# RWKV-5 attention and a tanh-shrink layer on one core: how many blocks of tokens take the early passes

## The chip, the core and the metric

The kernel runs on one core of a Trainium2 chip. A core has a matrix engine (PE, with its weight loads shown apart as PEld), a vector engine (DVE), an activation engine (ACT), a general engine (POOL), and SP, which here only issues transfers. Each runs its own list of instructions in order; semaphores tie them together. The metric is the device time of one launch in microseconds (us); lower is better.

## The reference

Three inputs r, k and v of 4 batches x 8 heads x 768 steps x 48, a decay w and a bonus u per head and channel, and two weight matrices.

```python
for t in range(S):
    kt, vt, rt = (k[:, :, t], v[:, :, t], r[:, :, t])
    cur = np.einsum('bhd,bhe->bhde', u[None] * kt, vt)
    y[:, :, t] = np.einsum('bhd,bhde->bhe', rt, state + cur)
    state = w[None, :, :, None] * state + np.einsum('bhd,bhe->bhde', kt, vt)
...
x = np.ascontiguousarray(attn_out.transpose(0, 2, 1, 3)).reshape(B * S, H * D)
h = x @ w_in
g = h - np.tanh(h)
return (g @ w_out).astype(np.float32)
```

x is 3072 x 384, w_in 384 x 2048, w_out 2048 x 384. The activations are fp32; w_in and w_out arrive as 64-bit floats, which the kernel converts itself.

## The kernel before, in words

**The work.** The attention is computed in 24 *units*, each 64 steps of two batches. Two units (L = 2) give 256 tokens, one *block* of the dense layer: 12 blocks. The dense layer's 2048 inner columns are cut into 16 slices f of 128, taken in pairs: a *tile* is one block with one pair of slices, and there are 12 x 8 = 96 tiles.

- **A unit** (`unit`, inside `near`): SP fetches r, k and v in six transfers (L730); DVE multiplies k by a decay table (kw, L871); PE transposes r and kw (L742); DVE scales r (rT, L746) and ACT copies k (kT, L755); PE multiplies rT with the running state and with kT (L697); DVE masks the result into `at` (L896), whose diagonal ACT has written (L767) from a product of r and k summed on DVE (L759, L886, L763); PE makes the outputs and the state's update (L697); ACT copies the outputs to the block's `xt` (L833); DVE updates the state (L860, L905). Some rows reach `xt` by six small transfers from POOL (L854).
- **A tile** (`hidden`): PE makes h in two halves of six matmul records (L167, `Dense.h`); ACT makes five functions of it (L176 to L184); DVE makes g in four steps (L191, L193, L195, L197); then PE multiplies g by w_out.
- **Plain or seven.** That last product is either four plain fp32 matmuls of 384 columns (L205, `Dense.o`), or a scheme of seven products of 192 columns (L255, `products`), as in Strassen's method. The seven need sums of g, which POOL makes (L240 to L244), and *mixed* sums of w_out, which DVE makes once all weights are converted (L264, `mix`). After a block's last seven-product tile the seven results are put together in seven steps, one on ACT (L274) and six on DVE (L283, `collect`), with the buffers e, u and o.
- **Weights.** 16 *pieces* (`Weights`), half of w_in and half of w_out, each 768 KB in HBM: loaded by SP and POOL (L122), converted by five steps on DVE (L136, L137, L140 to L142) and two on ACT (L138, L139). Every fourth pair of slices needs four pieces.

**The order of blocks.** All weights can't be there at the start. So the first FIRST = 5 blocks go through the dense layer in three *passes* over f, PASSES = 4, 4, 8 slices: two tiles of each of the five blocks, then again two of each, then four of each. The first two passes are plain and their sums are kept (`part`, L218 and L229); the third takes seven products and adds the kept sum (`gather`, L287). The other blocks, 5 to 11, go one after another with all eight tiles in seven products, but for the very last tile, which is plain.

The units of blocks 0 to FIRST + 1 (the first 14) use two banks of PSUM of their own (x_ps); units from 14 on (`two` in the code) share one pair of banks, and their product with the state is a step apart, followed by a small copy on ACT. The first seven-product tile needs the last of the first 14 units, since the seven results take over the x_ps banks.

**What sets the order of instructions.** `Plan` takes each step with an engine, a cost in us, and what it waits for. A fixed-seed search over due times fills an order per engine; the kernel issues exactly that order. Transfers carry another figure, `data`, the time for which each occupies the transfer channel: 3.0 for a w_out piece, 1.2 and 0.8 for the parts of a w_in piece on SP and POOL, 0.62 for half of a unit's r, k or v. Loads of weights are issued no sooner than 45 us before they are due (`gated`). Where the plan leaves PE idle before the first h and before the first o, *fillers* are put in (L632, a matmul of the identity with itself, in 512 or 256 columns). The plan also counts PE's instructions and expects PE to wait for its own at every 256.

**Buffers.** `xt` has FIRST + 2 buffers and `part` 2 x FIRST. In `collect`, e and u have 384 columns each, of which u uses 192; `kU`, used by unit 0 alone, lies in the buffers of `rk`.

Of the kernel before, what the change touches and what calls it, by code (L numbers as in the profile page):

```python
# [11 lines left out]
F32 = mybir.dt.float32  # L12
# [18 lines left out]
SHORT = 64  # L31
# [1 line left out]
PAD = 64  # L33
AHEAD = 2
L = 2
FIRST = 5
PASSES = 4, 4, 8
OWN = 1
SWAP = 2
# [105 lines left out]
class Dense:  # L145
# [62 lines left out]
    def empty(self, t, i):  # L208
# [13 lines left out]
        else:  # L222
            t.o = self.sums[at] = self.work.tile([128, self.d.DM], F32, name="part", tag="part", bufs=L * FIRST)
        if t.j == self.d.NB - 1:
# [41 lines left out]
    def collect(self, t, x):  # L266

        n, ps, V = self.d.DM // 2, self.seven.ps, self.nc.vector
        if x == 0:
            t.e, t.u = (self.work.tile([128, self.d.DM], F32, name=name, tag=name, bufs=1) for name in "eu")  # L270
            t.os = [self.work.tile([128, self.d.DM], F32, name="o", tag="o") for _ in range(L)]
            if t.fs[1] < self.d.NF:
                self.sums.update({(t.j, i): t.os[i] for i in range(L)})
            self.nc.scalar.copy(t.e[:, :n], ps[0][:, :n])  # L274
        else:
            o, e, u = t.os, t.e, t.u[:, :n]
            out, x, y, op = [(e[:, n:], e[:, :n], ps[0][:, n : 2 * n], ALU.subtract),
                             (u, e[:, n:], ps[1][:, n : 2 * n], ALU.add),
                             (o[1][:, :n], u, ps[1][:, :n], ALU.add),
                             (o[1][:, n:], u, ps[2][:, n : 2 * n], ALU.add),  # L280
                             (o[0], e, ps[2][:, : 2 * n], ALU.add),
                             (o[0][:, n:], o[0][:, n:], ps[3][:, :n], ALU.add)][x - 1]
            V.tensor_tensor(out, x, y, op)  # L283
# [15 lines left out]
class Plan:  # L299
# [7 lines left out]
    HOP, NEAR_HOP, LANDS, LANDED, LANES, EARLY, SPARE, WARM, SLOW = 0.16, 0.06, 2.4, 1.6, 8, 45.0, 20.0, 6.0, (60.0, 3.0)  # L307
    CHUNK, CHUNK_0, ASKED, COMES, FIRST = 256, 192, 55, 3.4, 9.5
    BEGIN = {"PE": 1.5, "DVE": 2.2, "ACT": 1.2, "POOL": 4.3, "SP": 1.2}
# [4 lines left out]
    def add(self, engine, cost, run, after=(), due=1e9, data=0, gated=False, steps=0):  # L314
        t = SimpleNamespace(engine=engine, cost=cost, run=run, after=[x for x in after if x], due=due, data=data,
                            gated=gated, steps=steps, then=[], n=len(self.tasks))
        for x in t.after:
            x.then.append(t)
        self.tasks.append(t)
        return t  # L320
# [12 lines left out]
    def forward(self, due):  # L333

        ready = [max(self.FIRST, due[t.n] - self.EARLY) if t.gated else 0.0 for t in self.tasks]
        count = [len(t.after) for t in self.tasks]
# [157 lines left out]
def near(ctx, tc, r, k, v, w, u, out, shared, moe_w_in, moe_w_out):  # L494
# [5 lines left out]
    H, D, NP, NK, B, HEAD = d.H, d.D, d.NP, d.NK, d.B, d.HEAD  # L500
# [4 lines left out]
    work = ctx.enter_context(tc.tile_pool(name="n_work", bufs=2))  # L505
# [10 lines left out]
    add = plan.add  # L516
# [149 lines left out]
    def steps(generator):  # L666

        made = []

        def step():  # L670
            if not made:
                made.append(generator())
            next(made[0])

        return step

    loads, converted = [], []
    for n in range(weights.count):

        queues, data = (("SP",), (3.0,)) if n % 4 > 1 else (("SP", "POOL") * 2, (1.2, .8) * 2)  # L680
        of = [add(e, .55, lambda n=n, i=i, e=e: weights.load(n, i, e_of[e]), [converted[n - 4] if n >= 4 else None],
                  data=x, gated=True) for i, (e, x) in enumerate(zip(queues, data))]
        if weights.sources[n % 4 > 1].dtype != I64:
            converted.append(of[-1])
            continue
        step = steps(lambda n=n: weights.convert(n))
        now = of + ([converted[n - 2]] if n >= 2 else [])
        for name, cost in (("DVE", .47), ("DVE", .47), ("ACT", .84), ("ACT", .84), ("DVE", .87), ("DVE", .87), ("DVE", .87)):
            now = [add(name, cost, step, now)]
        converted += now  # L690
# [10 lines left out]
    def unit(n):  # L701
# [6 lines left out]
        t = SimpleNamespace(at=ats[n % 2])  # L708
        rt, vt, kw, state = rts[n % (AHEAD + 1)], vts[n % (AHEAD + 1)], kws[n % 2], states[half]
        two = n >= L * (FIRST + 2)  # L710
        pair = yk_ps if two else x_banks[n == 1]
# [13 lines left out]
        def fetch(name, src, after):  # L725
            def run(z):
                if name == "k" and not hasattr(t, "kt"):
                    t.kt = first_k[slot] if direct else load.tile([128, H, D], F32, name="kt", tag="kt")
                to = {"r": rt, "v": vt}.get(name)
                Q.dma_start(out=(t.kt if to is None else to)[HALF[z], :, :D],  # L730
                            in_=src[half * 2 + z, :, steps_at, :].rearrange("h t d -> t h d"))

            of = [add("SP", .65, lambda z=z: run(z), after, data=.62) for z in range(2)]
            return add("none", 0, lambda: None, of)

        x.r = fetch("r", r, [b3.turn, b3.rk, b1.r])
        x.k = fetch("k", k, [b3.kw, b3.rk, b1.k])
        x.v = fetch("v", v, [b3.out, b1.v])

        def turn(src, to):  # L740
# [26 lines left out]
                A.mul(t.at[:, h % 2, h // 2], same, t.du[:, h : h + 1])  # L767

        def own_k():
            t.kU = work.tile([128, NP, 2, SHORT], F32, name="kU", tag="rk")  # L770
            for p in range(NP):
                A.mul(t.kU[:, p], t.kT[:, p], w_u[:, p : p + 1])

# [56 lines left out]
        def given(out, y):  # L830

            def copy(out, y):
                A.copy(out, y) if sign > 0 else A.activation(out, y, AF.Copy, scale=sign)  # L833

            if not swap:
                copy(out, y)
                return
            copy(out[:, 0], y[:, 0])
            for i in range(2):
                copy(out[i * PAD : (i + 1) * PAD, 1], y[to(i, 1), 1])  # L840

        def to_xt():
            if slot == 0:
                dense.xts[j] = work.tile([128, NK, L, C], F32, name="xt", tag="xt", bufs=FIRST + 2)
            given(dense.xts[j][:, :, slot].rearrange("e p (z t) -> e z p t", z=2), y_ps[:, :, :NK])
# [34 lines left out]
        if product:  # L880
            now = add("ACT", 1.05, own_k, [x.kT, w_us])
            x.own = add("PE", .7, own_levels, [now, x.rT, b2.out], steps=64)
            x.diag = add("DVE", .64, lambda: V.copy_predicated(t.at, same.bitcast(I32)[:, None, None, :].to_broadcast([128, 2, NP, SHORT]), own_lev), [x.own, b2.out])
        else:
            x.rk = add("DVE", .47, own, [x.r, x.k, b2.du, b1.rk if not b1.own else None])
            now = add("DVE", .47, lambda: V.tensor_tensor(t.rk, t.rk, ub, ALU.mult), [x.rk, bonus])  # L886
            x.du = add("DVE", .47, own_sum, [now, b2.diag])
            now = add("ACT", 1.0, lambda: diagonal(range(0, H // 2)), [x.du, b2.out])
            x.diag = add("ACT", 1.0, lambda: diagonal(range(H // 2, H)), [now])
# [9 lines left out]
        if direct:  # L899
            now = x.out = add("PE", .6, to_state, [now, x.kw], steps=64)  # L900
        x.xt = add("ACT", .96 if swap else .4, to_xt, [now, last_h.get(j - FIRST - 2) if slot == 0 else None])
        if not direct:
# [362 lines left out]
def kernel(  # L1265
# [29 lines left out]
    with tc.manual_schedule():  # L1295
        near(tc, r, k, v, w, u, out, shared, moe_w_in, moe_w_out)
# [39 lines left out]
```

## Time and profile before

| | |
|---|---|
| runs, us | 610.80, 610.86, 612.87 (median 610.86) |
| profiled execution | 610.4 us, of which the span of instructions is 608.7 |
| mean clock granted to PE | 0.992 |
| busy us: PE, PEld, DVE, ACT, POOL | 584.0, 497.8, 465.0, 403.4, 211.3 |
| PE's groups | h 1152 records, seven products 1050, plain o 168 (of 21 tiles), units 3200 with the transposes |
| read from HBM, written | 26.94 MB, 4.72 MB |

An fp32 matmul leaves two records in the profile, so h of one tile is 12 records. Matmuls overlap in the records: the ends are modelled, and the time from one start to the next tells more than a duration. Times within a profile are counted from the start of the span. "Issue" is a wait that nothing in the profile ended.

### The profile page before, as it was taken

The page shows a single profiled execution, that of the slowest core. Times are in us where ns is not written, and L with a number is a line of the kernel's source. Part 1 is how long each engine was busy: PE and PEld are TensorE (multiplying, and loading weights), DVE is VectorE, ACT ScalarE, POOL GpSimd, SP SyncE. Part 2 cuts the span into 40 slices and gives each one's busy share as a digit, 9 for nine tenths or more (in the row PEclk, how much of TensorE's full clock was granted, in tenths as well). Part 3 has the DMA queues.
Part 4 walks back from the last instruction along what each step waited for, and adds up shares of the span by engine and source line. Part 5 has one row for each costly group of instructions (what it writes and reads, how often), then busy time and mean ns, then how long its engine had stood idle before and what let it go on. Part 6 is the DMA issues. An engine that isn't in the chain of part 4 may idle for free.

```text
span 608.7 us, 14333 instructions
## 1 busy us (share of the span) xinstructions
PE 584.0 (96%) x5617; PEld 497.8 (82%) x5617; DVE 465.0 (76%) x771; ACT 403.4 (66%) x902; POOL 211.3 (35%) x384
## 2 busy tenths in 40 slices
PE   9789889999999989999999999999999999999994
PEld 5466667777777979999999888999889989899993
DVE  4789999999999999777765856875766875646753
ACT  2478979887786565666665765865676575765552
POOL 5001122010013454555463442453424432444430
PEclk9799999999999999999999999999999999999998
DMA  7998867653012020011020221310121100100101
GB/s 126 215 160 143 198 120 114 170 103 106 13 28 46 1 41 6 20 26 27 12 49 14 51 47 18 65 34 14 34 41 27 33 9 8 28 3 5 26 1 32
DMA packets 86325, 33.77 MB, mean 55 GB/s; under 512 B 78536, under 2 KB 80680, under 8 KB 86248
## 3 DMA queue, kind: packets, MB, share of 16 engines
q1 hardware_dynamic: 81084, 25.57, 22.2%
q0 software_dynamic: 4992, 6.99, 5.4%
q8 instruction: 46, 0.75, 0.5%
q14 instruction: 31, 0.25, 0.2%
q10 hardware_dynamic: 172, 0.20, 0.1%
HBM read 26.94 MB, written 4.72 MB: 52 GB/s over the span
## 4 chain that ended last, share of the span: by engine, by line
PE 69%; DVE 12%; ACT 8%; issue 7%; POOL 1%; DMA 1%; DVEq 0%; POOLq 0%; ACTq 0%
PE h L167 32%; PE p L255 24%; PE yk_ps L697 4%; PE o L205 4%; PE h L632 2%; DVE tg L193 1%; DVE tg L195 1%; DVE g L197 1%; DVE rT L746 1%; DVE g L191 1%; ACT th L178 1%; PE yk_ps L742 1%; ACT at L767 1%; POOL xt L854 1%; ACT s L176 1%
## 5 line engine op out<-in xcount | busy, mean ns | idle before, releaser
L167 PE MATMUL h<-xt,w_in_sb 128*128 128x256 f32 x1152 | 282.4, 382 | 0.1
L167 PEld LDWEIGHTS h<-xt,w_in_sb 128*128 128x128 f32 x1152 | 212.5, 190 | 30.1 <-issue 0.7
L240 POOL TENSOR_TENSOR sg<-g 128x256 f32<-128x256 f32 x75 | 57.0, 759 | 197.6 <-DVE g L197 142.6
L191 DVE TENSOR_TENSOR g<-h,th 128x512 f32<-128x512 f32 x96 | 66.2, 689 | 60.6 <-ACT s L176 26.8
L255 PE MATMUL p<-mixed,sg 128*128 128x192 f32 x450 | 110.1, 326 | 0.0
L180 ACT ACTIVATE tg<-h 128x512 f32<-128x512 f32 x96 | 57.3, 597 | 62.3 <-PE h L167 62.3
L193 DVE SCALAR_TENSOR_TENSOR tg<-s,tg 128x512 f32<-128x512 f32 x96 | 69.6, 725 | 25.1 <-ACT tg L180 13.8
L176 ACT ACTIVATE s<-h 128x512 f32<-128x512 f32 x96 | 57.6, 600 | 38.5 <-PE h L167 37.7
L178 ACT ACTIVATE th<-h 128x512 f32<-128x512 f32 x96 | 57.1, 595 | 37.7 <-PE h L167 37.7
L255 PEld LDWEIGHTS p<-mixed,sg 128*128 128x128 f32 x450 | 79.3, 190 | 0.2 <-issue 0.2
L255 PE MATMUL p<-w_out_sb,g 128*128 128x192 f32 x300 | 74.9, 332 | 1.3 <-DVE e L283 0.9
L197 DVE COPY_PREDICATED g<-small,tg 128x512 f32<-128x512 int32 x96 | 71.2, 742 | 4.3
L195 DVE SCALAR_TENSOR_TENSOR tg<-q,tg 128x512 f32<-128x512 f32 x96 | 68.7, 716 | 6.5 <-ACT q L182 2.3
L182 ACT ACTIVATE q<-s,m1b 128x512 f32<-128x512 f32 x96 | 69.6, 725 | 0.8
L184 ACT ACTIVATE small<-s,smallb 128x512 f32<-128x512 f32 x96 | 69.4, 723 | 0.5
L854 POOL DMA_DIRECT2D xt<-rest x66 | 32.1, 493 | 106.0 <-ACT rest L833 105.5
L255 PEld LDWEIGHTS p<-w_out_sb,g 128*128 128x128 f32 x300 | 54.9, 190 | 9.5 <-DVE e L283 1.3
L205 PE MATMUL o<-w_out_sb,g 128*128 128x384 f32 x160 | 59.1, 492 | 2.0 <-DVE g L197 1.2
L767 ACT ACTIVATE at<-same,du 128x64 f32<-128x64 f32 x184 | 47.5, 342 | 7.1 <-DVE du L763 7.0
L244 POOL TENSOR_TENSOR sg<-sg,g 128x128 f32<-128x128 f32 x75 | 44.4, 592 | 5.4
L205 PEld LDWEIGHTS o<-w_out_sb,g 128*128 128x128 f32 x160 | 29.3, 190 | 15.7 <-PE x_ps L632 1.6
L242 POOL TENSOR_TENSOR sg<-sg,g 128x128 f32<-128x128 f32 x75 | 40.2, 535 | 5.4
(129 smaller groups left out, 703.6 us busy)
## 6 DMA issues: line engine op xcount, KB each, us to landing
st<-in_moe_w_out_dram SPq DMA_DIRECT2D x8, 768.0 KB, 6.8
rt<-in_r_dram SPq DMA_DIRECT2D x48, 96.0 KB, 3.2
vt<-in_v_dram SPq DMA_DIRECT2D x48, 96.0 KB, 3.1
st<-in_moe_w_in_dram SPq DMA_DIRECT2D x16, 288.0 KB, 5.5
kt<-in_k_dram SPq DMA_DIRECT2D x44, 96.0 KB, 4.6
out_dram<-o POOLq DMA_DIRECT2D x44, 96.0 KB, 2.1
st<-in_moe_w_in_dram POOLq DMA_DIRECT2D x16, 96.0 KB, 5.7
xt<-rest POOLq DMA_DIRECT2D x66, 16.0 KB, 2.1
```

The lines of the kernel that those rows point to most:

```text
L167: self.nc.tensor.matmul(t.h2[:, z], self.w_in_sb[:, t.f // 2, kk, z * 128 : (z + 1) * 128], self.xts[t.j][:, kk].rearrange("p b t -> p (b ...
L176: A.activation(out, t.h, AF.Square)
L178: A.activation(out, t.h, AF.Tanh)
L180: A.activation(out, t.h, AF.Tanh, scale=G1)
L182: A.activation(out, t.s, AF.Square, bias=self.m1b)
L184: A.activation(out, t.s, AF.Relu, bias=self.smallb, scale=-1.0)
L191: V.tensor_tensor(t.g, t.h, t.th, ALU.subtract)
L193: V.scalar_tensor_tensor(t.tg, t.s, C4, t.tg, ALU.mult, ALU.mult)
L195: V.scalar_tensor_tensor(t.tg, t.q, K1, t.tg, ALU.add, ALU.mult)
L197: V.copy_predicated(t.g, t.small.bitcast(I32), t.tg)
L205: self.nc.tensor.matmul(self.outs[i], t.g2[:, z, i * C : (i + 1) * C], self.w_out_sb[:, t.f + z, :], start=t.first and z == 0, stop=t.last ...
L255: self.nc.tensor.matmul(ps[bank][:, half * n : (half + 1) * n], a, b, start=t.first and half == 0, stop=t.last, skip_group_check=True)
```

## The change

FIRST becomes 6: six blocks go through the three passes, and 16 units use the early banks. The tiles of the sixth block with f 0 to 6 thereby become plain and their sums are kept and gathered. `u` shrinks to the 192 columns in use (e keeps its 384), and `kU` moves from rk's buffers to q's. In the planner, half of a unit's r, k or v counts 0.71 us of the channel, and POOL's part of a w_in piece 0.95. The search runs with the same seed over the new steps, and the order that it returns is another from the first instructions on.

```diff
-FIRST = 5
+FIRST = 6
 PASSES = 4, 4, 8
...
         if x == 0:
-            t.e, t.u = (self.work.tile([128, self.d.DM], F32, name=name, tag=name, bufs=1) for name in "eu")
+            t.e, t.u = (self.work.tile([128, w], F32, name=name, tag=name, bufs=1) for name, w in (("e", 2 * n), ("u", n)))
...
-            o, e, u = t.os, t.e, t.u[:, :n]
+            o, e, u = t.os, t.e, t.u
...
-        queues, data = (("SP",), (3.0,)) if n % 4 > 1 else (("SP", "POOL") * 2, (1.2, .8) * 2)
+        queues, data = (("SP",), (3.0,)) if n % 4 > 1 else (("SP", "POOL") * 2, (1.2, .95) * 2)
...
-            of = [add("SP", .65, lambda z=z: run(z), after, data=.62) for z in range(2)]
+            of = [add("SP", .65, lambda z=z: run(z), after, data=.71) for z in range(2)]
...
-            t.kU = work.tile([128, NP, 2, SHORT], F32, name="kU", tag="rk")
+            t.kU = work.tile([128, NP, 2, SHORT], F32, name="kU", tag="q")
```

## The prediction

> **What bounds the kernel now.** I read the page's slices first, then the engines' busy time by stretch.
>
> ```profile
> PE   9789889999999989999999999999999999999994
> DVE  4789999999999999777765856875766875646753
> PEclk9799999999999999999999999999999999999998
> DMA  7998867653012020011020221310121100100101
> ```
>
> PE is at 9 nearly everywhere; the digits below 9 lie in the first six slices (15.2 us each) and in the last. DVE is at 9 up to slice 15 and then falls to 5 to 8: two regimes. The stretches (columns: length, then PE, PEld, DVE, ACT, POOL busy with counts, granted clock, DMA share, GB/s):
>
> ```profile
> 20.00:30.00 10.00, 7.04 (x94) 5.14 (x95) 6.26 (x11) 3.53 (x9) 1.01 (x2) 0.66 1.10 236
> ...
> 60.00:80.00 20.00, 16.79 (x344) 11.88 (x337) 19.40 (x36) 18.85 (x54) 2.88 (x6) 1.00 0.77 175
> 80.00:100.00 20.00, 18.77 (x320) 14.65 (x320) 18.08 (x31) 16.33 (x41) 4.93 (x10) 1.00 0.83 138
> 100.00:120.00 20.00, 19.66 (x261) 14.76 (x261) 19.85 (x35) 17.78 (x49) 2.92 (x6) 1.00 0.64 150
> ...
> 160.00:180.00 20.00, 20.00 (x144) 15.12 (x143) 20.00 (x33) 15.65 (x28) 0.00 (x0) 1.00 0.07 13
> ```
>
> From 110 us on, PE never stops for long: what counts there is the PE work itself. From 60 to 110 us DVE is full and PE waits for it, 4.8 us in all. Before that everything waits in turn: loads, DVE, and once PE's own instructions. PE in order of time there:
>
> ```profile
> 18.50 0.70 PE L632 MATMUL h<-ident 128*128 128x512 f32 x1
> 22.96 1.22 PE L632 MATMUL h<-ident 128*128 128x512 f32 x1 [3.76 <-issue]
> 24.11 0.92 PE L697 MATMUL yk_ps<-at,vt 64*64 64x64 f32 x24
> ```
>
> A single filler matmul is cut in two by a stop of 3.76 us that no engine ended, and the group behind it takes 0.92 us instead of the 0.58 of its first run: the clock stands at 0.50 for 6.8 us. ACT waits 6.0 us for the transposes behind this (kT L755 from PE x_ps L742), and DVE's rT waits for that.
>
> The price of a dense tile, from two places where PE runs without a gap (PE in order of time, then the chain):
>
> ```profile
> 137.25 1.46 PE L167 MATMUL h<-xt,w_in_sb 128*128 128x256 f32 x6
> 138.54 1.45 PE L205 MATMUL o<-w_out_sb,g 128*128 128x384 f32 x4
> 139.83 1.46 PE L167 MATMUL h<-xt,w_in_sb 128*128 128x256 f32 x6
> ```
>
> ```profile
> 254.22 1.29 PE h L167 x6
> 255.51 1.30 PE p L255 x8
> 256.81 1.29 PE h L167 x6
> 259.08 1.29 PE h L167 x6
> ```
>
> Starts count, since the ends overlap: a half of h or of a plain o is 1.29, so a plain tile is 5.17 us; a seven-product tile steps from 254.22 to 259.08, 4.86 us.
>
> [...] idle from 19.2 to 22.96, clock 0.50 from 21.6 to 28.4. [...] The trace has 46 such packets in 0.75 MB[...]; the second came at 19.9 us, amid a DMA share of 1.1, and was not hidden. [...]
>
> **The change part by part.** The order of instructions is fixed when the program is built, so I compare the two orders.
>
> *PE's work.* Four tiles (one block, f 8 to 14 unchanged, f 0 to 6 now plain) go from seven products to plain: 4 x (5.17 - 4.86) = +1.25 us. Units 14 and 15 now use the early layout, in which the groups with rT stand together: a joined pair costs 1.30 us between dense halves (156.63 to 157.82, and 0.11 in the next half), two single ones 0.83 each (330.16 to 330.88, and 0.11): 2 x -0.35 = -0.7. Fillers: 11 of 512 and 1 of 256 columns on h before, 7 and 5 after; 5 and 3 on x_ps before, 8 and 2 after: 18 and 18.5 of 512 altogether, nothing. PE's work: **+0.6 us**, all on the path.
>
> *What DVE lets PE do.* I summed DVE's instructions by their mean durations up to the copy_predicated (L197) that ends each tile's g; and PE's, without fillers, up to the first o of the same tile (0.216 us per h matmul of 256 columns, 0.324 per o, 0.52 to 0.56 per group of 32, 0.5 per four transposes). A tile costs DVE 2.87, a unit 5.03, a converted piece 4.00. Before, tile 1 ends at 50.45 with a sum of 39.3 and tile 12 at 136.33 with 136.9: DVE passes 1 us of sum in 0.88, neighbours overlapping. With that rate and the start as now, the tiles after end at 50.45 + 0.88 (sum - 39.3). "Lost" is the time at which o starts less PE's work ahead of it; after, its least value.
>
> ```
> tile  before: DVE sum, PE sum, o starts, lost | after: DVE sum, ends, PE sum, lost at least
>  1            39.3     19.3    50.6      31.3 |        43.2   53.9   22.4     31.7
>  2            48.7     32.0    64.2      32.2 |        54.9   64.2   30.8     33.6
>  4            71.7     42.7    78.4      35.7 |        72.6   79.8   46.1     33.9
>  8           112.1     76.9   115.8      38.9 |       109.7  112.4   79.6     33.0
> 11           131.9     94.3   133.4      39.1 |       133.1  133.0   98.4     34.8
> 16           162.4    122.5   161.8      39.3 |       161.3  157.8  126.7     31.3
> ```
>
> Before, lost time grows to 39.1 and stays: PE is saturated. After, DVE holds PE to 34.8 at most: six blocks draw 12 tiles from the first four pieces, so at tile 8 five pieces are converted instead of eight, and PE has more of the units behind it. Up to 4.3 us can go. But PE also waits for unit steps (1.8 us for state L860, 0.8 for at L767), and more units come early; before, lost time grew 7.8 between tiles 1 and 9, while the floor after grows 3.1. I take **-3.0 us**; bounds 0 (all of it becomes waits on units) and -4.3.
>
> *The start.* SP now issues w's rows first, not fourth (0.8 us instead of 3.0). The decay table follows them, so unit 0 can start up to 3 us earlier. But piece 0's conversion waits for its load, which landed at 19.34, the moment DVE took it; the loads ahead of it are the same to one. What can move is unit 2: its rT ran at 28.27, held by the stop and the slow clock, while its r had landed by 23.3. Counted through the orders, the stop falls after 220 matmul records; after the change that is still among the fillers ahead of unit 1's outputs, but with 2.5 fillers of 512 run instead of a half, 1.7 us more cover, and the block is asked for earlier if unit 0 is earlier. Without the stop, rT could run at about 24.5 to 25.5: with 0.9 us more DVE work ahead of it, up to 4.4 us of DVE's lead. The trace doesn't show whether PE, waiting for r until 23, loses its clock all the same. I take **-2.0**; bounds -4.4, and +3.4 if a stop of the same kind comes later (half of 6.8 us at half clock).
>
> *Costed at nothing.* Smaller e and u, kU in q's buffers: no instruction changes; q's last reader there is the scan at 8.8 us. DVE gains two adds (L218, 0.574) and two gathers (L287, 0.693), ACT two copies (0.475), all beside saturated PE; were PE to wait for them, 3.5 us. POOL loses 12 additions (7.5 us), and has room. The DMA figures act through the order alone: second-pass pieces are issued later on SP, behind seven more units' loads, whose buffers come free as units pass; DVE asks for them later too.
>
> Sum: 608.7 + 0.6 - 3.0 - 2.0 = 604.3 span. The profiled run took 610.4 for 608.7, so 606.0; the median of the runs stands 0.5 above it: **606.5**.
>
> **Rivals.** (1) *The stop goes wholly*: -4.4 instead of -2.0, so 604.1. For: the boundary has more before it and is asked for earlier. Against: r of unit 2 lands at 23 anyway. (2) *The lead is not used*: PE's waits for units replace those for g, and the start stays: only PE's +0.6 is left, 611.5. For: lost time grew in 60 to 80 us, where ACT is at 18.85 of 20 as well, and units are denser there after. (3) *Slower: the second pass's weights come late.* Piece 4 stands on SP behind unit 11's k, whose buffer waits for unit 8's kw on DVE, by the sums at about 73 us; it lands 5.5 us (the page's median for these loads) or more later, at about 80, and DVE reaches its conversion at about 87. If it slips by more than these 7 us, DVE stops in its queue with the tiles' steps behind it, and PE with it, each us one us: slower than now from 4.4 us beyond, and at 10 beyond, 606.5 + 10 = 616.5. For: a load of the first 30 us took up to 11.6 us to land. Against: DMA share is 0.8 there, and later loads than before leave the early ones room.
>
> **How the numbers follow.** Forecast (603.5 to 609): 0.45. Rival 1: 0.2; rival 2: 0.15; rival 3: 0.2. A measurement can tell about 0.5%, 3.1 us, so faster is below 607.8: three quarters of the forecast and rival 1, 0.53; same, 0.27, the rest and rival 2; slower, 0.2, rival 3. The range, 600.5 to 615.5, takes in the start's -4.4 with DVE's -4.3 at its low end and reaches toward rival 3 at its high end, since only two in ten may be left out.
>
> **What would show it.** Right: no gap over 0.5 us on PE from 70 us on until the first products; o of tile 8 starting near PE's sum plus 36; rT of unit 2 by 26 us. Rival 1: clock at 1.00 through 20 to 30 us. Rival 2: PE waiting for at or state at 60 to 110 us as much as now. Rival 3: L136 waiting for st. The forecast is wrong if the time from the first seven products to the end differs by more than the four tiles' 19.4 us and the units account for.

## The result, and the profile after

| | before | after |
|---|---|---|
| runs, us | 610.80, 610.86, 612.16, 612.87 (median 611.51) | 604.17, 604.63, 606.31, 606.58 (median 605.47) |
| profiled execution, its span, us | 610.4, 608.7 | 606.31, 604.5 |
| mean clock granted to PE there | 0.992 | 0.993 |

The ratio is 0.9898, 95% interval 0.9866 to 0.9929: about 6 us off. The profiled spans differ by 4.2. The runs of the changed kernel come in two pairs, at 604.2 to 604.6 us with a mean clock of 0.996 and at 606.3 to 606.6 with 0.993. The stretch at half clock in this profile takes 3.4 us (39.6 to 43.0), and 3.4 / 2 / 605 is 0.003 of mean clock, so one such stretch more or less would account for 1.7 of the 2 us; only an execution of the upper pair was profiled, so this is not shown. All times here are of fast executions: beside f1 to f4 below, two of the kernel before (625 and 861 us, mean clock 0.942 and 0.655) and two of f4 (1129 and 1172 us, 0.84 and 0.92) were slow and are left out.

The slices of the page after:

```profile
PE   7889998999999999999999999999999999999994
DVE  5789989999999999987667856756986665744753
PEclk9989999999999999999999999999999999999998
DMA  6986569572621210111011120131310100100101
```

The 7 in PEclk's second slice is gone; apart from the last slice, only the third shows an 8. DMA's digits in the third to fifth slices are smaller (8, 6, 5 for 9, 8, 8), and those in the seventh and ninth larger (9, 7 for 7, 5): part of the loading has moved later. The same stretches as before the change (length, then PE, PEld, DVE, ACT, POOL busy, clock, DMA share, GB/s):

```profile
20.00:30.00 10.00, 8.52 (x165) 6.24 (x169) 7.38 (x13) 5.73 (x17) 0.27 (x1) 1.00 0.96 199
...
60.00:80.00 20.00, 19.32 (x383) 14.61 (x383) 18.45 (x34) 17.41 (x54) 3.90 (x8) 1.00 0.50 98
80.00:100.00 20.00, 19.81 (x383) 15.00 (x382) 17.61 (x31) 19.35 (x56) 6.42 (x14) 1.00 0.89 168
100.00:120.00 20.00, 18.43 (x266) 13.96 (x259) 19.35 (x33) 16.51 (x37) 4.77 (x10) 1.00 0.73 144
```

PE now works 39.13 of the 40 us from 60 to 100, against 35.56; it does that with DVE less full, not more (36.06 against 37.48). PE's idle time there fell from 4.44 to 0.87 us. Its waits from 70 to 120 us, before and then after:

```profile
PE yk_ps L697 <- DVE state L860: 1.8, 1, 1.8
PE yk_ps L697 <- issue: 0.9, 1, 0.9
PE o L205 <- ACT at L767: 0.8, 1, 0.8
PE o L205 <- DVE g L197: 0.4, 1, 0.4
```

```profile
PE h L167 <- issue: 1.6, 1, 1.6
PE yk_ps L697 <- DVE state L860: 0.5, 2, 0.3
```

The waits for g and for ACT's part of `at` are gone; one of 0.3 us for DVE's part of `at` is left, between 60 and 70 us. PE in order of time, at the places that the prediction spoke of:

```profile
20.09 1.13 PE L632 MATMUL h<-ident 128*128 128x512 f32 x3 [0.43 <-issue]
...
38.27 0.69 PE L697 MATMUL yk_ps<-rT,state 48*64 48x64 f32 x32 [2.22 <-DVE state L860]
39.37 4.54 PE L167 MATMUL h<-xt,w_in_sb 128*128 128x256 f32 x12
...
101.73 1.46 PE L167 MATMUL h<-xt,w_in_sb 128*128 128x256 f32 x6 [1.57 <-issue]
```

The stop at 20 us shrank from 3.76 to 0.43. But the clock was halved all the same, later and for half as long: after the idle 2.22 us ahead of the state's product, it stands at 0.50 from 39.6 to 43.0, and the twelve records of h take 4.54 us, where the twelve at 25.17, at a clock of 1.00, take 2.83. A stop on instructions of 1.57 us comes at 100 us, and ends 1.4 us after a packet of the instruction queue has landed. DVE's rT of unit 2, before and after (one line of each kernel):

```profile
28.27 0.69 DVE L746 TENSOR_TENSOR rT<-x_ps,w_up 128x512 f32<-128x512 f32 x1 [2.23 <-ACT kT L755]
```

```profile
26.67 0.68 DVE L746 TENSOR_TENSOR rT<-x_ps,w_up 128x512 f32<-128x512 f32 x1
```

It runs 1.6 us earlier and waits for nothing. Unit 0's rT moved by as much, from 11.25 to 9.43: the earlier start, by 1.8 us, is enough to account for unit 2. These two profiles don't tell it from the shorter stop; f4 below does, for the changed kernel.

**Where the 4.2 us of span came from.** I count "lost" time as in the prediction, but at the end of a tile's h: the time reached less PE's useful work up to there.

| at the end of h of tile | 8 | 12 | 20 | 32 | 40 | 96 |
|---|---|---|---|---|---|---|
| before | 38.4 | 39.3 | 39.4 | 43.1 | 43.5 | 52.8 |
| after | 35.6 | 36.2 | 36.4 | 38.2 | 39.2 | 47.2 |

Lost time fell by 3.1 up to tile 12, by 1.8 more up to tile 32, gave 0.6 back up to tile 40, and fell by 1.3 more to the end: 5.6. PE's useful work is 1.3 longer (541.9 against 540.6). 5.6 - 1.3 = 4.3. Up to tile 12, 6.8 us ran at half clock before and 3.4 after, which can make up to 1.7 of the 3.1. The piece at tiles 12 to 32 is mostly the first collections of seven products. PE's waits over the whole span, before and then after:

```profile
PE p L255 <- DVE e L283: 0.9, 1, 0.9
...
PE p L255 <- DVE o L283: 0.8, 1, 0.8
```

```profile
PE p L255 <- DVE o L283: 0.3, 1, 0.3
```

### The profile page after: what moved, and what is told of

It reads as the page before. It is cut to its first block, busy times and chain, and to the rows that moved or that the text cites. A ratio compares the mean times of both kernels' runs of the same rounds, so it can differ in the third digit from the quotient of the medians.

```text
span 604.5 us, 14282 instructions
## 1 busy us (share of the span) xinstructions
PE 583.7 (97%) x5597; PEld 493.8 (82%) x5597; DVE 466.9 (77%) x775; ACT 403.6 (67%) x902; POOL 204.6 (34%) x372
## 4 chain that ended last, share of the span: by engine, by line
PE 81%; DVE 8%; ACT 5%; issue 2%; SPq 1%; DMA 1%; POOL 0%; ACTq 0%; DVEq 0%; POOLq 0%
PE h L167 38%; PE p L255 25%; PE o L205 9%; PE yk_ps L697 6%; DMA st<-in_moe_w_in_dram 1%; PE x_ps L742 1%; DVE rT L746 1%; SPq L730 1%; ACT kT L755 1%; PE yk_ps L742 1%; DVE tg L193 1%; PE x_ps L697 1%; ACT xt L833 1%; ACT s L176 1%; DVE tg L195 1%
## 5 line engine op out<-in xcount | busy, mean ns | idle before, releaser
L240 POOL TENSOR_TENSOR sg<-g 128x256 f32<-128x256 f32 x71 | 54.8, 772 | 178.4 <-DVE g L197 149.7
L191 DVE TENSOR_TENSOR g<-h,th 128x512 f32<-128x512 f32 x96 | 66.0, 688 | 50.8 <-ACT s L176 24.0
L255 PE MATMUL p<-mixed,sg 128*128 128x192 f32 x426 | 104.1, 326 | 0.2 <-issue 0.2
L176 ACT ACTIVATE s<-h 128x512 f32<-128x512 f32 x96 | 57.4, 598 | 41.1 <-PE h L167 40.8
L255 PEld LDWEIGHTS p<-mixed,sg 128*128 128x128 f32 x426 | 75.0, 190 | 0.4 <-issue 0.4
L255 PE MATMUL p<-w_out_sb,g 128*128 128x192 f32 x284 | 70.7, 331 | 0.1
L195 DVE SCALAR_TENSOR_TENSOR tg<-q,tg 128x512 f32<-128x512 f32 x96 | 67.2, 700 | 4.1 <-DVE tg L193 0.5
L205 PE MATMUL o<-w_out_sb,g 128*128 128x384 f32 x192 | 69.6, 488 | 0.0
L255 PEld LDWEIGHTS p<-w_out_sb,g 128*128 128x128 f32 x284 | 52.0, 190 | 7.4 <-DVE e L283 0.5
L205 PEld LDWEIGHTS o<-w_out_sb,g 128*128 128x128 f32 x192 | 35.6, 190 | 15.8 <-DVE part L218 0.3
L244 POOL TENSOR_TENSOR sg<-sg,g 128x128 f32<-128x128 f32 x71 | 40.7, 573 | 5.1
L242 POOL TENSOR_TENSOR sg<-sg,g 128x128 f32<-128x128 f32 x71 | 38.8, 547 | 5.4
```

The costliest lines, as they stand in the source:

```text
L176: A.activation(out, t.h, AF.Square)
L191: V.tensor_tensor(t.g, t.h, t.th, ALU.subtract)
L195: V.scalar_tensor_tensor(t.tg, t.q, K1, t.tg, ALU.add, ALU.mult)
L205: self.nc.tensor.matmul(self.outs[i], t.g2[:, z, i * C : (i + 1) * C], self.w_out_sb[:, t.f + z, :], start=t.first and z == 0, stop=t.last ...
L255: self.nc.tensor.matmul(ps[bank][:, half * n : (half + 1) * n], a, b, start=t.first and half == 0, stop=t.last, skip_group_check=True)
```

## The experiments

All runs share the table below. *Floor* is the prediction's sum, the largest of 50.65 + 0.88 (DVE's sum - 39.3) less PE's sum over tiles 1 to 16, worked out from the order of instructions alone; it is anchored at tile 1 of the kernel before and so is an estimate, not a strict bound. The lost time, and the time for which PE's clock stood at 0.50, are measured in each trace. The time is the median over 5 to 22 runs; the kernel before, beside them, stood at 611.7, 611.1 and 611.2.

| run | first blocks, seed, figures | floor | lost at tile 20 | at half clock up to tile 20 | lost from tile 40 to 96 | us |
|---|---|---|---|---|---|---|
| before | 5, 5, old | 39.3 | 39.4 | 6.8 | 9.3 | 611.5 |
| e2 | 5, 5, new | 43.1 | 41.0 | 10.2 | 9.0 | 611.24 |
| e4 | 5, 6, old | 37.7 | 36.2 | 0 | 8.4 | 606.29 |
| e6 | 5, 7, old | 38.6 | 40.9 | 10.2 | 8.0 | 606.88 |
| e8 | 5, 8, old | 36.2 | 38.2 | 6.8 | 9.7 | 610.36 |
| after | 6, 5, new | 34.8 | 36.4 | 3.4 | 8.0 | 605.47 |
| e1 | 6, 5, old | 36.9 | 38.2 | 3.4 | 6.9 | 607.67 |
| e3 | 6, 6, new | 35.4 | 35.9 | 3.4 | 6.3 | 608.51 |
| e5 | 6, 7, new | 37.0 | 45.3 | 13.7 | 6.5 | 612.64 |
| e7 | 6, 8, new | 36.3 | 36.5 | 6.8 | 8.0 | 606.44 |
| f1 | 4, 5, new | 48.0 | 52.6 | 27.3 | 11.8 | 622.96 |
| f2 | 4, 5, old | 40.2 | 40.8 | 13.7 | 9.0 | 611.69 |

**Blocks and figures apart.** e1 is the changed kernel with the old figures, e2 the kernel before with the new ones.

```diff
-            of = [add("SP", .65, lambda z=z: run(z), after, data=.71) for z in range(2)]
+            of = [add("SP", .65, lambda z=z: run(z), after, data=.62) for z in range(2)]
```

(and .95 to .8 in the load of w_in; e2 the other way round.)

> The change with the old DMA figures (0.62 and 0.8), so six blocks and the smaller buffers alone. Theory (six blocks draw more tiles from the first four pieces, so DVE holds PE less): the gain is there without the figures. Summed as in the prediction, the lost time is held to at most 36.9 (tile 11) instead of 34.8 for the whole change and 39.1 measured before, so about 606 to 609 us. Rival A (the gain comes from the DMA figures[...]): no gain, 610 to 613, with waits on loads or weights.

> The kernel before with the new DMA figures only, five blocks. Theory: no gain from the figures alone; the sums hold lost time to 41 to 43 (tiles 9 and 16), at or above the 39.1 of before, so 610 to 614 us. Rival A (the figures bring the gain): 604 to 607.

e1: 607.67, ratio to before 0.9941 (0.992 to 0.9962). e2: 611.24, ratio 0.9998 (0.9982 to 1.0013). The figures alone bring nothing to five blocks; six blocks alone bring 3.6 us, and with the figures 6. But each of these is one draw of the search, one order that it happens to return, and the next runs show how much that is worth.

**The same numbers, another draw.** The search's seed is changed and nothing else: e3, e5 and e7 are the changed kernel, e4, e6 and e8 the kernel before.

```diff
-        chance = Random(5)
+        chance = Random(6)
```

> The whole change, with another seed of the planner's search. Theory: six blocks gain whatever order the search finds; sums hold lost time to 35.4, so within 3 us of the change, 603 to 608. Rival B (the change only drew a luckier order): seeds scatter by as much as the change gained, and this one may well lie at 610 or above.

> The kernel before with the same other seed, five blocks, old figures. Theory: sums hold lost time to 37.7, a little under the 39.1 of before, so 608 to 612. Rival B: anywhere from 604 to 616, and as likely below the other-seed six-block kernel as above it.

e3 took 608.51 (ratio 0.995, 0.993 to 0.9969), e4 606.29 (0.992, 0.9891 to 0.9948): with this seed five blocks are the faster. So two more seeds for each.

> Six blocks with the new figures, a third seed of the search. The second seed left the change at 608.5 us and brought the five-block kernel to 606.3, so order alone moves several us. Theory as it now stands (six blocks take 1 to 3 us off on average, order moves single kernels by as much): sums hold lost time to 37.0, 605 to 609 us, and below the five-block kernel of the same seed. Rival B (only the order counts): no relation to five blocks; as likely above it as below.

> Five blocks with the old figures, the third seed. Theory: sums hold lost time to 38.6, so 608 to 612 us, 1 to 4 above the six-block kernel of this seed. Rival B: 604 to 612, no relation to it.

> Six blocks with the new figures, a fourth seed. Theory: sums hold lost time to 36.3, so 604 to 608 us, below the five-block kernel of this seed. Rival B: as likely above it as below.

> Five blocks with the old figures, the fourth seed. Theory: sums hold lost time to 36.2, as low as for six blocks here; five blocks has 1.3 us less PE work and about 0.7 more for two late units, so 605 to 609 us, within 2 us of the six-block kernel of this seed. Rival B: 604 to 612.

e5: 612.64 (1.0018, 1.0002 to 1.0034). e6: 606.88 (0.9913, 0.9883 to 0.9943). e7: 606.44 (0.9921, 0.9889 to 0.9953). e8: 610.36 (0.9979, 0.9967 to 0.9992). The whole change less the kernel before is -6.0, +2.2, +5.8 and -3.9 by seed: a mean of -0.5, with a standard error of 2.7. Over all five orders of each count, old and new figures together, the means are 608.1 and 609.3, a difference of -1.1 with a standard error of 1.7. That six blocks gain whatever the order is refuted by two seeds of four; that they take 1 to 3 us off in the mean is neither shown nor ruled out by so few draws. A draw of the order alone moves the time by up to 7 us, more than the whole change did.

The worst draw, e5, shows a case that no sum of busy time contains. PE's waits in e5 between 30 and 70 us:

```profile
PE yk_ps L697 <- DVE state L860: 3.9, 2, 2.9
PE yk_ps L697 <- DVE at L896: 0.9, 1, 0.9
PE x_ps L742 <- DVE at L896: 0.9, 1, 0.9
```

PE is busy for 34.10 of these 40 us and DVE for 32.02: they wait for each other by turns within the units. The floor says 37.0, and 45.3 are lost. A floor counts what an engine has to do, not the length of a unit's own chain. Nor does it count the clock: 13.7 us of e5 up to tile 20 ran at half clock, after this stretch's idle time and an earlier stop of 4.7, which can account for up to 6.8 of the 8.3 us. The traces don't part the two.

**Four blocks.** f1 takes FIRST = 4 with the new figures, f2 with the old ones.

```diff
-FIRST = 5
+FIRST = 4
```

> Four blocks first instead of five, with the new DMA figures (0.71, 0.95). By the same sums as in the prediction, DVE ends g of tile 8 so late in this order that PE must have lost at least 48.0 us when it starts o of tile 8 (five blocks: 39.3, six: 34.8). If DVE's sums set a floor, the time lost up to tile 12 is 48 or more, and the time is 611.5 + 8.7 - 0.6 of PE's work + 1.8 for two more late units = 621. If the sums say nothing and only the draw counts, as the seeds suggest, lost is 35 to 45 and the time 606 to 613.

> Four blocks first, everything else as in the kernel before. The floor from DVE's sums is 40.2 (five blocks: 39.3), PE's work is 0.6 less, and 12 units instead of 10 come late. If each late unit costs 0.9 us of waiting, as the runs of five and six blocks have it (8.9 and 7.2 us lost between tiles 40 and 96), 10.7 us are lost between tiles 40 and 96, and the time is about 613.5, give or take 3 for the draw. If the number of late units does not matter, 7 to 9 are lost there and the time is 606 to 612.

f1 took 622.96 (1.0199, 1.0171 to 1.0227), beside 621 worked out ahead from DVE's sums. Two stretches of f1:

```profile
60.00:80.00 20.00, 16.75 (x303) 12.83 (x303) 17.94 (x31) 15.33 (x42) 5.28 (x10) 0.78 0.88 167
80.00:100.00 20.00, 16.70 (x309) 12.15 (x308) 19.36 (x34) 16.19 (x45) 2.92 (x6) 1.00 0.64 137
```

DVE is nearly full and PE is not: 33.45 of 40 us, where the changed kernel has 39.13; and in the first stretch PE's clock averaged only 0.78. Part of the nearness to 621 is luck: the lost time at tile 20 is 4.6 above the floor, and some 2 us less than in the kernel before are lost from there to tile 40. f2, whose floor is 40.2 and so nearly the kernel before's, took 611.69 (1.0011, 0.9995 to 1.0027), with 40.8 lost at tile 20. So the sums tell an order's lost time roughly: in eleven of the twelve orders it lies between 2.1 below and 4.6 above the floor; e5 is the exception. What the sums tell is a property of the order drawn, only loosely one of the number of blocks.

A rival stands beside the floor. The time at half clock up to tile 20 runs from 0 in e4 to 27.3 us in f1 (the table), and over the twelve orders the lost time follows it more closely (correlation 0.95) than it follows the floor (0.82); without f1 the two are 0.86 and 0.48. Half clock came after idle time of PE (3.76 us before, 2.22 after), and what came behind took longer (4.54 us instead of 2.83 for the h above), so these runs don't say how much of an order's loss is the one or the other.

The late part does go with the number of blocks. Call the units outside the early banks late: from tile 40 to 96, 7.1 us are lost in the mean of the five orders with six blocks (8 late units) and 8.9 with five blocks (10 late units), a difference of 1.7 with a standard error of 0.5, so some 0.9 a late unit. The two orders with four blocks (12) have 11.8 and 9.0, in the mean 10.4. f2, at 9.0 instead of the 10.7 expected, lost no more than an order with five blocks does: alone, it fits as well that the number doesn't matter.

**Borders of instruction blocks.** f3 is the kernel before, f4 the changed kernel, each with 24 products of 1 x 1 ahead; the order that follows is the same, 96 PE instructions further on (24 x 4: the two records that an fp32 matmul leaves, and as many weight loads; the page before counts 5617 of each).

```diff
+    for _ in range(24):
+        T.matmul(idle[0:1, 0:1], shared["one"], shared["one"], start=True, stop=True)
     for t in plan.order():
```

> The kernel before with 24 products of 1 x 1 ahead of PE's first instruction, so that the borders of the blocks in which PE's instructions come lie 96 instructions earlier; the order is the same. If the stop of 3.76 us and the half clock after it hold unit 2 up, as the prediction's term for the start has it, the block is asked for earlier, the stop shrinks below 1.5 us, rT of unit 2 runs by 26.5 instead of 28.3, and the time is 607.5 to 609.5. If DVE's queue or the loads would hold unit 2 anyway, it stays at 611.5, within 0.5; the same if the block cannot land earlier, and then the stop only moves.

> The changed kernel with the same 24 products ahead. Its stop near 20 us is only 0.43 and has little to give; the stop of 1.57 us near 101 us, where PE is saturated, moves to another place. If such stops on a saturated PE cost their full length, 603.9 to 604.5; if the stops fall elsewhere in the same length, 605.5; if the first border now falls where the block has not landed, up to 3 us more.

f3 took 613.1 (1.0024, 1.0012 to 1.0037): slower by 1.9, where I expected a gain or nothing. PE in order of time in f3:

```profile
23.50 0.66 PE L697 MATMUL yk_ps<-vt,kw 64*64 64x48 f32 x13 [3.75 <-issue]
...
31.35 0.43 PE L697 MATMUL yk_ps<-vt,kw 64*64 64x48 f32 x10 [1.15 <-issue]
```

The stop didn't shrink: it is 3.75 again, at an earlier point of the order and at nearly the same time, and its block was moved at 20.48 us where it was 19.93 before. So in this order, where the block's border lies doesn't set the length of the stop: PE goes on 1.6 us after the block has landed, before the change as in f3. What f3 changed was something that I hadn't meant to. The 24 products took 1.34 us, the ten records of fillers behind them ran from 2.34 on and for 7.53 us instead of from 1.52 on and for 6.01, and the first transposes of r moved from 7.37 to 9.70. Unit 0's rT came 2.33 us later (13.58), unit 2's 3.4. The end of h of tile 12 came 2.0 later (132.9 against 130.9), and that of tile 96 1.9 (595.4 against 593.5). In this one order, **a delay of the start came out at the end at some 0.8 to one**, counted from unit 0. It is not a clean rate: f3 has two smaller stops besides, of 1.15 and 0.42 us, which may hold a part of it.

f4 took 606.76 (0.9932, 0.9906 to 0.9957), 1.3 above the changed kernel; with five runs against four, and these in pairs 2 us apart, I don't call that a difference. Its profiled execution has 606.34 and a clock of 0.993, and is compared with that of the changed kernel (606.31, 0.993). Its early stop is longer here, 1.11 us for 0.43, but ends 3 us earlier, at 17.10; and unit 2's rT comes 0.65 later, just as unit 0's does (10.08 for 9.43):

```profile
27.32 0.68 DVE L746 TENSOR_TENSOR rT<-x_ps,w_up 128x512 f32<-128x512 f32 x1
```

So in the changed kernel unit 2 follows the start and not the stop. The stop of 1.57 at 100 us is gone in f4, and from tile 10 on the ends of h agree within 0.1 us with the changed kernel. DVE in the changed kernel is 0.77 ahead of f4 near 100 us (L905) and 0.08 ahead near 109 (L860), having waited 0.43 for PE's transposes between. So that stop seems to have cost about 0.7 us, not its length; a reading of two traces, since the start moved too. No version that I ran is faster than the changed kernel.

## Why the prediction was right, and where it wasn't

The time, 605.47, is 1.0 from the 606.5 on record, and the profiled span is 604.5 where the sum gave 604.3. That it came so near is in part luck: the start and DVE's relief were to bring 5.0 us together, and 3.1 were won up to tile 12; some 1.2 came from tiles 12 to 40, where nothing was priced, and late units brought more than their price. Term by term:

- **PE's four tiles, +1.25:** right. In the changed kernel halves of plain tiles again step by 1.29 (115.44, 116.73, 118.03), and the work summed at these prices differs by 1.3.
- **Two units in the early layout, -0.7:** right in sign, too small. I priced only the matmul groups (0.35 a unit); with the waits that go with a late unit, it is some 0.9 a unit over the ten orders with five and six blocks, and in this pair -1.3 for the two.
- **The start, -2.0:** the mechanism was only half what I had written. rT of unit 2 ran at 26.67, not "by 26", and 1.6 us earlier; unit 0's rT was earlier by 1.8, as w's rows were issued first and the decay table's first step on DVE ran at 5.74 instead of 8.37. With f3's rate of 0.8, 1.8 us earlier would be worth -1.5, an estimate. I had put most of it down to the stop of 3.76 us. The stop did shrink, and rival 1's sign, a clock of 1.00 from 20 to 30 us, is there; yet the gain of 4.4 isn't: unit 2 moved by 1.6 only, and PE later idled 2.22 us for unit 3's state and had half clock at 39.6. So rival 1 fails though its sign came true. One reading was loose as well: the block that PE stopped for is the first of the 46 packets of the instruction queue in the trace, not the second. It was moved at 19.93 before and at 17.28 after, so earlier, as the prediction had it; that the earlier unit 0 is the reason isn't shown.
- **DVE's relief, -3.0:** up to tile 12 the lost time fell by 3.1 for both terms; less 1.5 for the start, 1.6 is left for this one. That is a remainder, half of the term, and the shorter half clock may be in it too. o of tile 8 started at 115.4 with a sum of 79.6 ahead of it, 35.8 lost: the "plus 36" that was named. The sums take DVE's instructions as equally long in both kernels, as L191 was (689 ns before, 688 after). DVE's sums pointed the right way (f1 above all, some 11.7 us slower and foretold as 10), but I took them for something that six blocks bring. Not all of the 4.8 us that I read as PE waiting for DVE from 60 to 110 us was that: 0.8 was for ACT, and 0.9 a stop on instructions. Five blocks with other seeds have floors of 36.2 to 38.6 in place of 39.3; the relief in this pair is in part a less lucky draw before and a lucky one after.
- **Not priced:** the collections. Two stalls of 0.9 and 0.8 us at the first ones became one of 0.3, 1.4 of the 1.8 us won between tiles 12 and 32. The prediction has only the gathers behind them, as a possible loss. Over the seeds, the time lost from tile 20 to 40 is 1.5 to 7.2 with six blocks and 2.2 to 5.7 with five; so this too is the draw.
- **Rival 2 (lead not used, 611.5)** didn't occur. **Rival 3 (second pass's weights late)** neither: DVE's waits for weights in the changed kernel are one of 0.9 and one of 0.5 us, both before 30 us.
- **No gap over 0.5 us from 70 us on:** one, the 1.57 us at 100 us, which by f4 cost about half of that. It is a stop "of the same kind" that the prediction had as a bound, though without the half clock that it priced.
- **The time from the first seven products to the end** fell from 411.1 to 382.8, by 28.3. The four tiles and PE's work of the two units and of h between the two places come to 24.8 by the orders. The remaining 3.5 us are waits: by the sign that I had named, the forecast missed a part, the collections and the late units.

So the size is right, and of the 5.6 us of lost time that went, 3.1 lie where the two large terms had put them. What failed is the step "Up to 4.3 us can go", as a claim about six blocks: the order that the search happens to return moves more than the block count does. The kernel after is faster than the kernel before; that six blocks as such are faster than five is not shown (-1.1 us, standard error 1.7). What is shown is that with six blocks 1.7 us less are lost in the late part (standard error 0.5), of which 1.25 are paid back in plain tiles. Whether they also ease DVE's early load in the mean stays open: floors average 36.1 with six blocks and 39.0 with five, but the lost times at tile 20 average 38.5 and 39.1, because of e5. It also stays open what decides when a block of instructions is moved; PE's stops ended 1.3 to 2.0 us after one had landed.

## What to carry to other kernels

Where a search or a planner orders the work, give each setting several seeds before crediting the setting: here one draw was worth up to 7 us, and the change 6. Sums of each engine's work up to a few checkpoints, taken from the order alone, picked out the one bad order here, f1, ahead of its run. Among the other eleven they are a loose guide (correlation with the time 0.52): they miss the idle turns of a chain that goes back and forth between two engines, and what a low clock adds. Time given back at the start need not reach the end in full: measure how much of it does by a known delay, in more than one order, as f3 did by accident in one.

## What the runs showed of the hardware

**Stops for instructions.** Before and after the change, the trace has 46 packets of 16 KB, 0.75 MB in all, on an instruction queue; one of these is what is called a block here. That they hold PE's instructions is read from the stops. In the first 25 us PE stopped so in ten of the twelve orders: for 3.8 us before, 0.4 after, 5.3 in e1, 0.8 in e3, 1.6 in e4, 4.7 in e5, 1.5 in e6, 1.7 in e7, 4.8 in e8, 2.7 in f2; none in e2 and f1. In these ten, and in f3 and f4, the stop falls ahead of PE's 220th or 221st matmul record, whatever the order. All 19 stops of over 0.3 us on PE that no engine ended, in the fourteen traces, ended 1.3 to 2.0 us after a 16 KB packet of the instruction queue had landed (before: 1.6 and 1.5; after: 1.3 and 1.4). Before the change the packet of the first stop took 1.41 us. The DMA share from 15 to 25 us was 1.0 to 1.2 in all (1.15 before, 1.05 after), with such a stop or without, so the share alone doesn't tell its length. A stop of 1.57 us on a PE that was busy 19.81 of the 20 us ahead of it cost, by f4, about half of its length.

**Half clock.** Up to tile 20 it came in stretches of 3.4 us (after), 6.8 (before) and twice 13.7 (f1). Idle stretches of 2.2 us (after) and 3.8 (before) were followed by one, and before the change the clock fell 2.4 us after the stop had begun. But in these traces the length of a single idle stretch doesn't tell: in e6 stretches of 1.8 and 1.5 us were followed by half clock, while one of 2.7 in e6, 2.2 in e3 and 2.3 in f1 were not.
